# Where weights' forms, probabilities and tokens' forms are made at the change of layer and of batch, in a fused attention and two-layer mixture kernel

## The chip, the cores and the metric

One core of one Trainium2 chip runs the whole kernel in one launch. The metric is device time in microseconds (us). The engines are TensorE (PE; its weight loads are PEld), VectorE (DVE), ScalarE (ACT), GpSimd (POOL) and SyncE (SP), which here issues all DMAs in one queue.

## What is computed

```python
def reference(**kwargs):
    # 2 batches, 8 heads, 768 tokens, 64 per head; local window and global keys
    attn_out = _attn_ref(**attn_kwargs)
    x = attn_out.transpose(0, 2, 1, 3).reshape(B * S, H * D)     # 1536 x 512
    # layer 1: w_gate, w_val 512 x 1536, w_out 1536 x 512
    gate = 1.0 / (1.0 + np.exp(-(x @ w_gate)))
    x = gate * (x @ w_val) @ w_out
    # layer 2: 4 experts, w1 512 x 1024 and w2 1024 x 512 each
    p = domain_probs / (domain_probs.sum(-1, keepdims=True) + 1e-09)
    for e in range(4):
        h = np.maximum(x @ w1[e], 0.0)
        out += p[:, e:e + 1] * (h @ w2[e])
```

## The kernel before

Every float32 product on PE is made of three products of parts: an operand is split into a part rounded to fp32r ("hi", a cast on ACT) and the rest ("lo", a difference on DVE or POOL), and `mm3` (L221) and `mm_on` (L226) multiply hi by hi, hi by lo and lo by hi. Each engine works through its own instructions in the order in which the program issues them; an order is written by hand, in places with generators whose `next` puts one more piece of side work between products.

**Layer 1** (`Experts.run`, L323) has NF // 2 = 6 steps j. In a step, six gates (`gate`, L296: two columns blocks f, three token chunks c of 512) each make 24 products into two banks of PSUM (pg, pv), then a sigmoid on ACT (L309), the gating gf on DVE (L316), its hi on ACT (L319) and lo on POOL (L320). Then twelve second blocks (`second`, L331: three chunks c, four row blocks d) each make six products into a bank po, which DVE adds to `parts` (L345). All of pg, pv and po share the four banks of `ps_mm`. Layer 1's own weights are loaded, decoded and split by `Weights`, a piece at a time ("chores"). In the last step, j = 5, the third chunk (c = 2) is kept for the end: its gates come after the second blocks of the first two chunks, and its four second blocks, a list `last`, are run inside round 0 of layer 2.

**Layer 2** (`Mixed`, L386) works in 32 rounds n: 16 (NG) for each of the two batches, 256 of the experts' columns in each. The product of tokens and w1 is made by a scheme with seven half-size products instead of eight (`PAIRS`, L384: product m takes weight form x and token form y). A round (L529) has seven such products of six matmuls of 384 columns each, on banks a, e and b (b is `o_all`); ACT copies b out twice (s2, L593, and s3, L597) before PE may go on adding into it, and DVE makes c22 (L598) and c12 (L611) from e. Between them stand six token tiles of the round before (`out_tile`, L508: six matmuls of 512 columns, pw, which DVE weighs with the probability and adds up, L524).

- *Weights' forms:* `load` (L406) brings w1's piece ("a") and w2's piece ("b"). `sums` (L414) makes four sums of w1's quarters on DVE (L422), `halves` (L432) splits three pieces into hi (ACT, L435) and lo (POOL or DVE, L436), of 512, 256 and 1024 columns. `outer` (L438) splits w2's piece (ACT, L442; POOL, L443; 1024 columns), which the token tiles of the next round need. In round n >= 1 the forms of round n+1 are made with `ahead`, and `outer(n)` stands near the end.
- *Tokens' forms:* `token_sums` (L449) makes four differences on DVE (L457), `token_form` (L459) splits one form (ACT, L461; DVE or POOL, L462) into a place of `xall`. There are eight places of 768 columns, and seven forms; the places of layer 1's tokens are used again. The forms of batch 0 are made by `begin` (L464) in the last step of layer 1, those of batch 1 inside round 15, each into its old place once the last product of batch 0 that reads it has run.
- *Probabilities:* `token_weights` (L127) loads `pr` (L128) and divides by its sum with four small operations on DVE (L129 to L132).

Before, all of this stood close to the change: at the second-last gate of j = 5 the program issues `load(0)`, `load(1, "a")` and `token_weights`; `begin` puts `sums(0)` behind the first second block of j = 5, then the three pieces, then the token forms; round 0 makes the sums and pieces for round 1 with DVE.

```python
L361  if (f, c) == (NF - 1, 1):
L364      mixed.load(0)
L365      mixed.load(1, "a")
L366      token_weights()
```

Of the kernel before, what the change touches and what calls it, by code (L numbers as in the profile page):

```python
# [18 lines left out]
P = 128  # L19
# [34 lines left out]
def tile_attention_moe(ctx, tc, q, k, v, n_global, n_local, w_gate, w_val, w_out, probs, w1, w2, out):  # L54
# [229 lines left out]
    class Experts:  # L284
# [38 lines left out]
        def run(self):  # L323
# [54 lines left out]
            last = [lambda d=d: (second(NF // 2 - 1, b, NCH - 1, d), next(forms, None)) for d in range(KD)]  # L378
            mixed.run([lambda i=i: [f() for f in last[i:i + 2]] for i in (0, 2)], forms, self.rest)
# [3 lines left out]
    ORDER = (0, 1, 3, 4, 5, 6, 2)  # L383
    PAIRS = {1: (0, 0), 2: (1, 1), 3: (6, 2), 4: (2, 6), 5: (3, 3), 6: (4, 4), 7: (5, 5)}  # L384

    class Mixed:  # L386

# [9 lines left out]

        def more_pools(self):  # L400
# [5 lines left out]
        def load(self, n, which="ab"):  # L406
            e, f0 = divmod(n % NG * 256, F2)
            for x in which:
                src = w1[e, :, f0:f0 + 256] if x == "a" else w2[e, f0:f0 + 256, :]
                t = (wr if n % 2 == 0 else self.rx if x == "a" else self.ry).tile([P, BW], F32, tag="raw", name=f"raw{x}")  # L410
# [3 lines left out]
        def sums(self, n):  # L414
# [8 lines left out]
            pool = self.wf[n % 2]  # L423
            self.forms[n] = [pool.tile([P, 7, KH, P], F32R, tag=x, name=f"w{x}") for x in ("hi", "lo")]
            flat = "p q k f -> p (q k) f"
            self.pieces = [
# [3 lines left out]
            ]  # L430

        def halves(self, i, eng=nc.gpsimd):  # L432

            src, hi, lo = self.pieces[i]
# [24 lines left out]
        def token_form(self, i, eng):  # L459
            hi, lo = (form_slot(i)[:, x] for x in range(2))  # L460
            nc.scalar.copy(hi, self.tsrc[i])  # L461
            eng.tensor_tensor(out=lo, in0=self.tsrc[i], in1=hi.bitcast(F32), op=ALU.subtract)  # L462

        def begin(self, pool):  # L464
# [10 lines left out]
            yield  # L475
            yield
            next(sums)
            self.token_form(3, nc.vector)
            yield
            next(sums)  # L480
            yield
            self.token_form(4, nc.vector)
            yield
            next(sums)
            self.token_form(2, nc.gpsimd)
            yield
            next(sums, None)

            for _ in range(2):
                yield  # L490
            for i in (5, 6):
                yield
                self.token_form(i, nc.vector)

        def product(self, ps, n, m, first):
            x, y = PAIRS[m]
            hi, lo = self.forms[n]
            t = form_slot(y)
# [30 lines left out]
        def round(self, n, fill):  # L529

            b, (s2, s3), (c22, c12) = self.b, *((x[:, :TH] for x in y) for y in (sgs, gfs))
            more = n + 1 < B * NG
            renew = iter(((0, nc.vector), (1, nc.gpsimd), (3, nc.vector), (4, nc.gpsimd), (5, nc.vector), (6, nc.gpsimd), (2, nc.gpsimd))
                         if n % NG == NG - 1 and more else ())
            fill = iter(fill)

            def fills():
                next(fill, lambda: None)()

            def ahead(i, eng=nc.gpsimd):  # L540

                if more and i == 0:
                    self.sums(n + 1)
                if more:
                    self.halves(i, eng)

            def renewed():
                for i, eng in renew:
                    self.token_form(i, eng)
                    break  # L550

            for f in range(2):
# [466 lines left out]
```

## Time and profile before

| what | value |
|---|---|
| median of 3 runs | 925.94 us (925.74 to 927.41) |
| profiled execution, its own time | 925.25 us |
| span, first to last instruction | 923.4 us |
| instructions | 12563 |
| PE busy | 896.4 us, 97% |
| DVE busy | 578.4 us, 63% |
| ACT busy | 393.5 us, 43% |
| POOL busy | 389.5 us, 42% |
| mean granted TensorE clock | 0.990 of full speed |

Busy time counts an instruction from its start to its end, and matmuls overlap one another, so a busy PE is not PE at its peak. A wait is idle time of an engine that ended with an event of another; where several were awaited it is put down to the last. Times in the timeline are counted from the start of the span. Attention and the start of layer 1 take the first 130 us, layer 1 lasts to about 413, with the first products of layer 2 from 402.6, and the change of batch, round 15 to 16, is near 656.

### The profile page before, as it was taken

How to read it: one execution, taken by the hardware profiler on the slowest of the kernel's cores; microseconds unless marked ns; L12 is line 12 of the kernel's file. 1: busy time of each engine (PE TensorE's matmuls, PEld its weight loads, DVE VectorE, ACT ScalarE, POOL GpSimd, SP SyncE). 2: the span in 40 equal slices, each digit the busy share in tenths (PEclk: the TensorE clock that was granted, in tenths of full speed). 3: DMA queues.
4: the chain of work that ended last, by engine and by line, in shares of the span. 5: the costliest groups of instructions: out<-in, count | busy, mean ns of one | idle time of the engine just before them, and what ended most of it. 6: DMA issues, size and time to landing. Idle time of an engine off the chain costs nothing.

```text
span 923.4 us, 12563 instructions
## 1 busy us (share of the span) xinstructions
PE 896.4 (97%) x4736; PEld 771.4 (84%) x4736; DVE 578.4 (63%) x1053; ACT 393.5 (43%) x778; POOL 389.5 (42%) x301
## 2 busy tenths in 40 slices
PE   7989999999999999899999999999899999999997
PEld 5777688888888888688989898989789898989896
DVE  6988653473746465667666666687866666666554
ACT  6989835323232221234343444434443434444331
POOL 2766443333333333333444444445744454444431
PEclk8999999999999999999999999999999999999999
DMA  9633312121121210102212131313132121312102
GB/s 194 155 86 73 109 50 91 46 92 46 65 73 46 92 46 24 46 18 95 72 52 86 46 91 46 92 46 92 57 117 78 47 90 46 92 47 92 46 23 72
DMA packets 83301, 66.46 MB, mean 72 GB/s; under 512 B 43168, under 2 KB 72096, under 8 KB 83232
## 3 DMA queue, kind: packets, MB, share of 16 engines
q1 hardware_dynamic: 83232, 65.57, 24.4%
q8 instruction: 39, 0.64, 0.3%
q14 instruction: 30, 0.25, 0.1%
HBM read 62.42 MB, written 3.15 MB: 71 GB/s over the span
## 4 chain that ended last, share of the span: by engine, by line
PE 87%; DVE 4%; ACT 3%; POOL 2%; issue 2%; DMA 1%; SPq 0%; DVEq 0%; POOLq 0%; ACTq 0%
PE pw L223 9%; PE pw L224 9%; PE pw L222 9%; PE o_all L228 4%; PE o_all L229 3%; PE o_all L230 3%; PE pg L222 3%; PE po L222 3%; PE po L223 3%; PE pv L222 3%; PE po L224 3%; PE pv L224 3%; PE pg L224 3%; PE pv L223 3%; PE pg L223 3%; PE pe L228 2%
## 5 line engine op out<-in xcount | busy, mean ns | idle before, releaser
L524 DVE SCALAR_TENSOR_TENSOR parts<-pw,pr,parts 128x512 f32<-128x512 f32 (+1 forms) x181 | 135.3, 748 | 123.5 <-PE pw L224 123.4
L223 PE MATMUL pw<-olo,h 128*128 128x512 f32 (+1 forms) x386 | 151.5, 393 | 1.4 <-POOL olo L443 1.4
L224 PE MATMUL pw<-ohi,h 128*128 128x512 f32 (+1 forms) x386 | 151.7, 393 | 0.0
L222 PE MATMUL pw<-ohi,h 128*128 128x512 f32 (+1 forms) x386 | 150.5, 390 | 0.0
L443 POOL TENSOR_TENSOR olo<-rawb,ohi 128x1024 fp32r<-128x1024 f32 x32 | 77.2, 2413 | 152.1 <-ACT ohi L442 152.1
L320 POOL TENSOR_TENSOR g<-gf,g 128x512 fp32r<-128x512 f32 x36 | 56.2, 1561 | 135.9 <-ACT g L319 130.7
L436 POOL TENSOR_TENSOR wlo<-sums,whi 128x1024 fp32r<-128x1024 f32 x31 | 74.5, 2402 | 64.6 <-ACT whi L435 64.6
L436 POOL TENSOR_TENSOR wlo<-rawa,whi 128x512 fp32r<-128x512 f32 (+1 forms) x62 | 67.9, 1117 | 64.6 <-ACT whi L435 64.6
L224 PEld LDWEIGHTS pw<-ohi,h 128*128 128x128 f32 x386 | 72.4, 188 | 15.7
L223 PEld LDWEIGHTS pw<-olo,h 128*128 128x128 f32 x386 | 72.6, 188 | 10.8 <-POOL olo L443 2.2
L222 PEld LDWEIGHTS pw<-ohi,h 128*128 128x128 f32 x386 | 72.5, 188 | 8.8
L228 PE MATMUL o_all<-x,whi 128*128 128x384 f32 x194 | 66.3, 342 | 2.7 <-ACT sg L593 2.1
L316 DVE TENSOR_TENSOR gf<-pv,sg 128x512 f32<-128x512 f32 x36 | 24.9, 691 | 66.1 <-PE pv L224 66.1
L229 PE MATMUL o_all<-x,whi 128*128 128x384 f32 x194 | 65.5, 338 | 0.0
L230 PE MATMUL o_all<-x,wlo 128*128 128x384 f32 x194 | 65.4, 337 | 0.0
L505 ACT ACTIVATE h<-gf 128x384 fp32r<-128x384 f32 x64 | 33.7, 527 | 73.3 <-DVE gf L611 52.2
L319 ACT CAST g<-gf 128x512 fp32r<-128x512 f32 x36 | 22.5, 624 | 96.5 <-DVE gf L316 96.5
L806 POOL TENSOR_SCALAR st<-st,rs 128x256 f32<-128x256 f32 (+1 forms) x96 | 48.6, 522 | 34.8 <-DVE rs L799 18.6
L222 PE MATMUL po<-g,whio 128*128 128x512 f32 x144 | 56.9, 395 | 3.4 <-DVE parts L345 2.2
L222 PE MATMUL pg<-x,whig 128*128 128x512 f32 x144 | 57.5, 399 | 0.0
L223 PE MATMUL po<-g,whio 128*128 128x512 f32 x144 | 56.9, 395 | 0.0
L222 PE MATMUL pv<-x,whig 128*128 128x512 f32 x144 | 56.8, 394 | 0.0
(145 smaller groups left out, 2130.9 us busy)
## 6 DMA issues: line engine op xcount, KB each, us to landing
rawa<-in_moe_w_dram SPq DMA_DIRECT2D x32, 512.0 KB, 5.0
rawb<-in_moe_w_dram SPq DMA_DIRECT2D x32, 512.0 KB, 4.0
bitsg<-in_moe_w_gate_dram SPq DMA_DIRECT2D x12, 512.0 KB, 3.7
bitsg<-in_moe_w_val_dram SPq DMA_DIRECT2D x12, 512.0 KB, 4.7
bitso<-in_moe_w_out_dram SPq DMA_DIRECT2D x6, 1024.0 KB, 4.9
v<-in_v_dram SPq DMA_DIRECT2D x12, 256.0 KB, 4.0
out_dram<-parts SPq DMA_DIRECT2D x11, 256.0 KB, 3.0
kn<-in_k_dram SPq DMA_DIRECT2D x10, 256.0 KB, 3.2
```

What stands on the lines that cost most here:

```text
L222: nc.tensor.matmul(ps, ah, bh, start=first, stop=False)
L223: nc.tensor.matmul(ps, ah, bl, start=False, stop=False)
L224: nc.tensor.matmul(ps, al, bh, start=False, stop=last)
L228: nc.tensor.matmul(ps, ah, bh, start=first, stop=False, skip_group_check=True)
L229: nc.tensor.matmul(ps, ah, bl, start=False, stop=False, skip_group_check=True)
L230: nc.tensor.matmul(ps, al, bh, start=False, stop=last, skip_group_check=True)
L320: nc.gpsimd.tensor_tensor(out=g[:, 1], in0=gf, in1=g[:, 0].bitcast(F32), op=ALU.subtract)
L436: eng.tensor_tensor(out=lo, in0=src, in1=hi.bitcast(F32), op=ALU.subtract)
L443: nc.gpsimd.tensor_tensor(out=lo, in0=raw, in1=hi.bitcast(F32), op=ALU.subtract)
L505: nc.scalar.activation(out=hi, in_=of, func=AF.Relu)
L524: nc.vector.scalar_tensor_tensor(out=at, in0=pw, scalar=p_e, in1=at, op0=ALU.mult, op1=ALU.add)
L806: nc.gpsimd.tensor_scalar(out=st, in0=st, scalar1=me["rs"][:, 2 * p + j:2 * p + j + 1], scalar2=1.0, op0=ALU.mult, op1=ALU.mult)
```

## The change

- The DMA of `pr` is issued at the start of `Experts.run`; the four operations on it stand at the start of step j = 1, with the load of the first w1 piece.
- `sums(0)` and the three pieces of round 0 are made in step j = 4, one after each of its first four gates (`begin_weights`). `sums` and `halves` are separated from the allocation of the forms' tiles.
- `begin` then makes only token forms, in another order (0, 1, 4, 3, 2, 5, 6) and a little later, and ends with `sums(1)`.
- The last four second blocks are no longer inside round 0: the two products 1 of round 0 come first (`first_products`), then the second blocks, then `first_round` with an order of products of its own (6, 2, 7, 5, 4, 3), in which the pieces of round 1 are split on ACT and POOL, `outer(0)` stands after the first of them, and the second half of `load(2)` at the end.
- The buffers of w1's and w2's pieces are exchanged: `wr` now holds w2 of even rounds and w1 of odd ones.
- Batch 1's token forms get places shifted by one (`slots`): form 0 goes into the spare eighth place, form 1 into form 0's, and so on along `ORDER`. Their sums are made in rounds 9 to 12 (before: 12 to 15), form 0 in round 13, forms 1, 3, 4 and 5 in round 15 with DVE and 6 and 2 with POOL (before: 0, 3 and 5 with DVE; 1, 4, 6 and 2 with POOL).
- In round 15 `outer` stands right after the first product, not near the end.

```diff
     def token_weights():
-        nc.sync.dma_start(out=pr, in_=probs.rearrange("(t p) e -> p t e", p=P))
         nc.vector.tensor_reduce(prs, pr, AX.X, ALU.add)
...
+            nc.sync.dma_start(out=pr, in_=probs.rearrange("(t p) e -> p t e", p=P))
             for j in range(NF // 2):
                 final = j == NF // 2 - 1
+                if j == 1:
+                    token_weights()
+                    mixed.load(0, "a")
+                early = mixed.begin_weights() if j == NF // 2 - 2 else iter(())
                 for f in fs:
                     for c in range(NCH - final):
                         if (f, c) == (NF - 1, 1):
...
-                            mixed.load(0)
+                            mixed.load(0, "b")
                             mixed.load(1, "a")
-                            token_weights()
                         gates(f, c, self.weights.chore)
+                        next(early, None)
...
-            last = [lambda d=d: (second(NF // 2 - 1, b, NCH - 1, d), next(forms, None)) for d in range(KD)]
-            mixed.run([lambda i=i: [f() for f in last[i:i + 2]] for i in (0, 2)], forms, self.rest)
+            mixed.first_products()
+            for d in range(KD):
+                second(NF // 2 - 1, b, NCH - 1, d)
+                next(forms, None)
+            for _ in forms:
+                pass
+            self.rest.close()
+            mixed.run()
...
+            order = (7,) + self.ORDER
+            self.slots = [{i: i for i in self.ORDER}, {i: order[k] for k, i in enumerate(self.ORDER)}]
...
-                t = (wr if n % 2 == 0 else self.rx if x == "a" else self.ry).tile(...)
+                t = (wr if (n % 2 == 0) == (x == "b") else self.rx if x == "a" else self.ry).tile(...)
...
+        def begin_weights(self):
+            self.sums(0)
+            for i in range(3):
+                yield
+                self.halves(0, i)

         def begin(self, pool):
             sums = self.token_sums(0, pool, "bits")
             next(sums)
-            self.sums(0)
+            for _ in range(3):
+                yield
+            self.token_form(0, 0, nc.vector)
             yield
-            for i in range(3):
-                self.halves(i)
+            self.token_form(0, 1, nc.vector)
+            for _ in range(3):
                 yield
-            self.token_form(0, nc.vector)
-            self.token_form(1, nc.vector)
...
+            for i in (None, 4, 3, None, 2):
+                if i is None or i == 4:
+                    next(sums, None)
+                if i is not None:
+                    self.token_form(0, i, nc.gpsimd if i == 2 else nc.vector)
+                yield
...
+            self.sums(1)
...
+        def first_round(self):
+            a, e = self.first
+            self.more_pools()
+            self.load(1, "b")
+            self.load(2, "a")
+            self.halves(1, 0)
+            self.outer(0)
+            self.product(b, 0, 6, False)
+            nc.scalar.copy(s2, b)
+            self.product(a, 0, 2, False)
+            self.gated(0, 0, 0, a, nc.vector)
+            self.halves(1, 2)
+            self.product(b, 0, 7, False)
+            nc.scalar.copy(s3, b)
+            self.product(e, 0, 5, True)
+            nc.vector.tensor_tensor(out=c22, in0=e, in1=s3, op=ALU.add)
+            self.product(b, 0, 4, False)
+            self.gated(0, 1, 0, b, nc.vector)
+            self.halves(1, 1)
+            self.product(e, 0, 3, False)
...
+            self.load(2, "b")
...
         def round(self, n):
-            renew = iter(((0, nc.vector), (1, nc.gpsimd), (3, nc.vector), (4, nc.gpsimd), (5, nc.vector), (6, nc.gpsimd), (2, nc.gpsimd))
-                         if n % NG == NG - 1 and more else ())
+            renew = iter(zip(self.ORDER[1:], (nc.vector,) * 4 + (nc.gpsimd,) * 2) if n == NG - 1 else ())
...
             self.product(a, n, 1, True)
+            nc.scalar.copy(b, a)
+            if n == NG - 1:
+                self.outer(n)
             renewed()
             fills()
...
-            if n == NG - 4:
+            if n == NG - 7:
                 self.sums_ahead = self.token_sums(1, self.ts, "ts")
                 next(self.sums_ahead)
-            if NG - 4 <= n < NG:
+            if NG - 7 <= n < NG - 3:
                 next(self.sums_ahead, None)
+            if n == NG - 3:
+                self.token_form(1, 0, nc.vector)
...
-            if n:
+            if n != NG - 1:
                 self.outer(n)
```

## Rows read from the trace of the kernel before

**Rows 1.** The page, part 1: busy time, share of the span, instructions.

```profile
PE 896.4 (97%) x4736; PEld 771.4 (84%) x4736; DVE 578.4 (63%) x1053; ACT 393.5 (43%) x778; POOL 389.5 (42%) x301
```

**Rows 2.** PE's waits, whole span: releaser: us in total, times, longest.

```profile
PE po L222 <- DVE parts L345: 2.2, 1, 2.2
PE o_all L228 <- ACT sg L593: 2.1, 2, 1.1
...
PE pw L223 <- POOL olo L443: 1.4, 1, 1.4
...
PE po L222 <- DVE gf L316: 1.2, 1, 1.2
...
PE o_all L228 <- ACT sg L597: 0.6, 1, 0.6
PE pe L228 <- DVE gf L598: 0.4, 1, 0.4
```

**Rows 3.** Windows: stretch, its length, busy (x instructions) by engine, granted clock, DMA share, GB/s.

```profile
150.00:200.00 50.00, 50.00 (x222) 41.42 (x221) 22.99 (x29) 17.29 (x28) 16.83 (x9) 1.00 0.20 64
304.51:326.28 21.77, 21.77 (x98) 18.03 (x97) 9.28 (x10) 6.26 (x9) 7.21 (x4) 1.00 0.16 50
375.23:391.71 16.48, 13.08 (x49) 9.99 (x48) 12.52 (x21) 4.08 (x6) 6.46 (x5) 0.90 0.20 55
385.00:390.00 5.00, 4.11 (x11) 3.23 (x12) 5.00 (x8) 2.62 (x3) 2.39 (x1) 0.68 0.00 0
391.71:402.60 10.89, 10.89 (x50) 9.01 (x49) 7.79 (x10) 4.13 (x6) 4.23 (x2) 1.00 0.01 2
402.60:404.72 2.12, 2.12 (x13) 2.12 (x12) 0.69 (x1) 1.10 (x2) 0.40 (x1) 1.00 0.00 0
412.52:419.56 7.04, 5.03 (x25) 4.07 (x24) 6.80 (x10) 4.66 (x8) 2.37 (x1) 1.00 0.74 227
623.83:641.96 18.13, 18.13 (x92) 16.34 (x90) 13.64 (x19) 7.49 (x14) 7.27 (x5) 1.00 0.25 67
639.52:660.73 21.21, 18.71 (x91) 16.22 (x90) 19.08 (x22) 12.44 (x21) 15.51 (x9) 1.00 0.17 52
```

**Rows 4.** Timeline of SP's DMA queue, 372 to 380: start, us, engine, line.

```profile
373.98 0.51 SPq L128 DMA_DIRECT2D pr<-in_moe_domain_probs_dram  x1
```

**Rows 5.** Timeline of DVE, 372 to 388; in brackets idle time before, and releaser.

```profile
379.05 0.20 DVE L129 TENSOR_REDUCE prs<-pr 128x12 f32<-128x48 f32 x1 [5.43 <-DMA pr<-in_moe_domain_probs_dram]
...
379.89 0.69 DVE L316 TENSOR_TENSOR gf<-pv,sg 128x512 f32<-128x512 f32 x1
...
381.08 0.42 DVE L422 TENSOR_TENSOR sums<-rawa 128x256 f32<-128x256 f32 x1
...
385.15 2.54 DVE L345 TENSOR_TENSOR parts<-po,parts 128x512 f32<-128x512 f32 x5
```

**Rows 6.** Timeline of POOL, 636 to 655.

```profile
637.40 2.41 POOL L443 TENSOR_TENSOR olo<-rawb,ohi 128x1024 fp32r<-128x1024 f32 x1 [4.53 <-ACT ohi L442]
...
648.78 2.44 POOL L436 TENSOR_TENSOR wlo<-sums,whi 128x1024 fp32r<-128x1024 f32 x1 [1.77 <-ACT whi L435]
651.18 2.57 POOL L462 TENSOR_TENSOR x<-tsum,x 128x768 fp32r<-128x768 f32 x1
```

**Rows 7.** Timeline of DVE, 640 to 653.

```profile
642.01 0.96 DVE L462 TENSOR_TENSOR x<-parts,x 128x768 fp32r<-128x768 f32 x1 [1.07 <-ACT x L461]
...
647.22 0.41 DVE L422 TENSOR_TENSOR sums<-rawa,sums 128x256 f32<-128x256 f32 x1
...
649.54 2.49 DVE L457 TENSOR_TENSOR tsum<-parts,tsum 128x768 f32<-128x768 f32 x1
```

**Rows 8.** Timeline of ACT in round 0.

```profile
412.49 1.05 ACT L442 CAST ohi<-rawb 128x1024 fp32r<-128x1024 f32 x1 [3.10 <-PE po L223]
```

**Rows 9.** Timeline of ACT in round 15.

```profile
641.14 0.84 ACT L461 CAST x<-parts 128x768 fp32r<-128x768 f32 x1
```

**Rows 10.** The page, part 5: line, engine, operation, busy and mean ns, idle before.

```profile
L524 DVE SCALAR_TENSOR_TENSOR parts<-pw,pr,parts 128x512 f32<-128x512 f32 (+1 forms) x181 | 135.3, 748 | 123.5 <-PE pw L224 123.4
```

More of the change, by code (lines that the diff above doesn't have):

```diff
@@ L527, in out_tile, with ahead @@
                     nc.sync.dma_start(out=out[row:row + P, ds], in_=at)
-        def round(self, n, fill):
-            b, (s2, s3), (c22, c12) = self.b, *((x[:, :TH] for x in y) for y in (sgs, gfs))
-            more = n + 1 < B * NG
-            renew = iter(((0, nc.vector), (1, nc.gpsimd), (3, nc.vector), (4, nc.gpsimd), (5, nc.vector), (6, nc.gpsimd), (2, nc.gpsimd))
-                         if n % NG == NG - 1 and more else ())
-            fill = iter(fill)
-            def fills():
[L538 to L545, printed above, removed]
+        def ahead(self, n, i, eng=nc.gpsimd):
+            if n < B * NG:
+                if i == 0:
+                    self.sums(n)
+                self.halves(n, i, eng)
@@ new lines, in banks, with first_products @@
+        def banks(self, n):
+            for f in range(2):
+                self.h[n, f] = self.hp[n % 2].tile([P, 2, TB], F32R, tag="h", name="h")
+            return [ps_t.tile([P, C], F32, tag="t", name=x)[:, :TH] for x in ("pa", "pe")]
+        def first_products(self):
+            self.first = self.banks(0)
+            self.product(self.first[0], 0, 1, True)
+            self.product(self.b, 0, 1, True)
+        def first_round(self):
+            b, (s2, s3), (c22, c12) = self.b, *((x[:, :TH] for x in y) for y in (sgs, gfs))
+            a, e = self.first
[17 more added lines that the diff above has]
+            self.product(e, 0, 3, False)
+            nc.vector.tensor_tensor(out=c12, in0=e, in1=s2, op=ALU.add)
+            self.gated(0, 0, 1, c12, nc.vector)
+            self.gated(0, 1, 1, c22, nc.vector)
+            self.load(2, "b")
@@ L547, in renewed, with round @@
+        def round(self, n):
+            b, (s2, s3), (c22, c12) = self.b, *((x[:, :TH] for x in y) for y in (sgs, gfs))
+            renew = iter(zip(self.ORDER[1:], (nc.vector,) * 4 + (nc.gpsimd,) * 2) if n == NG - 1 else ())
+            fill = iter(range(TT))
+            def fills():
+                self.out_tile(n - 1, next(fill))
             def renewed():
                 for i, eng in renew:
-                    self.token_form(i, eng)
+                    self.token_form(1, i, eng)
@@ L550, in renewed @@
                     break
-            for f in range(2):
-                self.h[n, f] = self.hp[n % 2].tile([P, 2, TB], F32R, tag="h", name="h")
-            a = ps_t.tile([P, C], F32, tag="t", name="pa")[:, :TH]
-            e = ps_t.tile([P, C], F32, tag="t", name="pe")[:, :TH]
+            a, e = self.banks(n)
             self.product(a, n, 1, True)
-            if n == 0:
-                self.product(b, n, 1, True)
-            else:
-                nc.scalar.copy(b, a)
+            nc.scalar.copy(b, a)
@@ L573, in round @@
             renewed()
[L574 to L575 removed]
+            self.ahead(n + 1, 2)
             fills()
[L577 to L587 removed]
+            if n == NG - 7:
                 self.sums_ahead = self.token_sums(1, self.ts, "ts")
                 next(self.sums_ahead)
[L590 removed]
+            if NG - 7 <= n < NG - 3:
                 next(self.sums_ahead, None)
+            if n == NG - 3:
+                self.token_form(1, 0, nc.vector)
             self.product(b, n, 6, False)
@@ L614, in round, with run @@
             self.gated(n, 0, 1, c12, nc.vector)
-        def run(self, fill, forms, rest):
-            self.rest, self.first = rest, forms
-            for n in range(B * NG):
-                self.round(n, fill)
-                fill = [lambda n=n, t=t: self.out_tile(n, t) for t in range(TT)]
-            for tile_out in fill:
-                tile_out()
+        def run(self):
+            self.first_round()
+            for n in range(1, B * NG):
+                self.round(n)
+            for t in range(TT):
+                self.out_tile(B * NG - 1, t)
     def head_rows(src, b, s0, n):
```

64 lines of the change are left out of this document (19 added, 45 removed).

## The prediction, made before the change was timed

> **What bounds the kernel now.** I read the shares of busy time first: PE is busy for 97% of the span [rows 1], so only time in which PE stands still, or runs slowly, can be won. The list of PE's waits says where it stands [rows 2]: leaving the attention aside, its entries name one of two places, the change of layer (releasers L345, L316, L593, L597, L598) and the change of batch (L593 once more, L443). Then I cut the span into stretches whose work can be compared [rows 3]. From 375.23 to 391.71 PE issues the 48 products of eight second blocks; from 391.71 to 402.60 it issues 48 products of the same size without a gap, in 10.89 us. The first stretch took 16.48, so 5.59 us are lost in it: 1.2 and 2.2 of waiting [rows 2], and 2.2 mostly in products at a lowered clock, since after the two gaps the granted clock shows 0.68 of full speed between 385 and 390, a mix of the levels 1.2 and 2.4 GHz [rows 3]. In round 0, the 24 products from 412.52 to 419.56 took 7.04; 12 of that size took 2.12 at 402.60, so 24 need 4.24 and 2.80 are lost. At the change of batch I compare 639.52 to 660.73, which is round 15 with the first product and token tile of round 16, with 623.83 to 641.96, the same work one round earlier: 21.21 against 18.13, so 3.08 are lost [rows 3]. Together 11.5 us can be won at these two places, and no more.
>
> **Change of layer, the probabilities.** The DMA of pr is issued at 373.98 [rows 4]; DVE, which has the reduction of pr next in its order, stands idle for 5.43 until it has landed at 379.05 [rows 5]. Behind it stands gf L316, whose bank of PSUM PE wants: the wait of 1.2. The change issues this DMA ahead of layer 1, on SP with nothing there to wait for, and the four small operations at the start of its second step (j = 1). They take 0.84, from 379.05 to the next operation at 379.89 [rows 5], and in 150 to 200, which holds the start of j = 1, DVE is busy 22.99 of 50 while PE never stands [rows 3]: I cost them at nothing. Without that cover they would cost at most their 0.84.
>
> **Change of layer, the weights' sums and forms.** Four sums run on DVE from 381.08 to 385.15, and the additions L345 that free PE's banks stand behind them [rows 5]: the wait of 2.2. They move, with three casts on ACT and three differences on POOL, behind the first four gates of j = 4. Those gates, 304.51 to 326.28, leave DVE busy 9.28 and POOL 7.21 of 21.77 [rows 3], so the sums' 4.07 and about 4.3 on POOL (an estimate by columns, 1792 against 1024 in the 2.44 of [rows 6]) find room. What queues behind them are weights of the second blocks, which begin two gates after this stretch, at 337. I cost the move at nothing; without cover, 4.07. What is late next in 375 to 391? DVE has eight additions left and three passes over 768 columns, which stand singly between additions; PE has four banks, so a delay of 0.96 [rows 7] reaches no product. Both gaps go, and with them the low clock: 5.59. Bounds 3.4, if the clock falls for other reasons, and 5.6.
>
> **Change of layer, round 0.** The new order makes two first products, four second blocks, then the other products, with the weight pieces of round 1 made on POOL instead of DVE and their sums made before. PE's first wait in the old round was for the copy s2 L593, behind the casts L442 and L435 on ACT; L442 itself had waited 3.10 for PE's last second block, whose memory it takes over [rows 8]. It still does. But s2 now stands behind that one cast of 1.05 [rows 8], and PE has two products (b6 and a2, 2.12) before b7 needs the copy. So about 0.2 remains of the 2.80; bounds 0 and 0.6 (the cast of a piece, if it waits for the same memory). Saved: 2.6. The layer change gives 5.6 + 2.6 = 8.2, bounds 5.6 and 8.4.
>
> **Change of batch, what goes.** The token sums move from rounds 12 to 15 to rounds 9 to 12, and form 0 to round 13, into the spare place. Round 14 carried such a pass with PE busy 18.13 of 18.13 [rows 3]: nothing. The shifted places let each form be made one product earlier; no row shows PE waiting for a form: nothing. Outer(15) moves to the head of round 15, so olo is ready when round 16 asks for it: the wait of 1.4 [rows 2] goes.
>
> **Change of batch, what comes.** The outer's cast now stands on ACT ahead of the cast of form 1, and its difference on POOL ahead of everything. Before, the first form's cast began at 641.14 and its difference ran on DVE from 642.01 to 642.97 [rows 7, 9]. Now the outer's cast (1.05) begins there, form 1's cast ends at about 642.9, and POOL has begun the outer's difference, 2.41 long [rows 6], at 642.25. What DVE does meanwhile is seen at 649.54: a subtraction of two SBUF operands, of the size that takes 0.96, took 2.49 and ended at 652.03, 0.81 after POOL's operation of 648.78 had ended at 651.22 [rows 6, 7]. So form 1's difference ends at 644.66 + 0.81 = 645.5, 2.5 later than its counterpart. A token tile (0.75 [rows 10]) and the sums for round 16 follow. Before, the sums ended at 647.63 [rows 7], with a form on POOL among them that is gone now; I take about 1.7 back for it and put their end at 648.55, 0.9 later. Their cast and s2 stand behind them on ACT, so PE's wait of 1.1 for s2 [rows 2] grows to about 2.1, and product b7 starts at 650.0.
>
> A second wait comes new. After the sums DVE has a gated difference, forms 3 and 4, a tile, form 5, a tile, then c22, for which product e3 waits. POOL's piece (2.44) and its form 6 (taken as 2.0; 2.57 at 651.18 with a wait in it [rows 6]) fall between these. From 648.55: 0.5 + 0.9, blocked to 652.4, 0.8 + 0.7, blocked to 655.1, then 0.8 + 0.7 + 0.5 gives 657.0 (operations of 384 columns at half of 0.96). PE, from 650.0, has two products of 1.06 and two tiles of 1.36 [rows 3] and wants c22 at 654.9: another 2.1. So round 15 loses about 4.3 against 3.08 before: **+1.2**. Bounds: 1.2 lost in all, if the sums end as before and DVE's forms get ahead of POOL's work, and 4.3: a gain of 1.9 and a loss of 1.2.
>
> The Trainium skill, SBUF — State Buffer, section "SBUF: two separate sides", says that a DVE operation with two SBUF inputs and a GpSimd operation exclude each other for a whole instruction, whichever starts first. The trace agrees, by the 0.81 above. By that rule the earlier outer on POOL speaks against the change, at +1.2; if the two only shared the port, form 1's difference would at most double, end by 644.0, and both waits would stay under 1: the change of batch would gain about 1.
>
> **The sum.** The profiled execution took 925.25 us (span 923.4): 925.25 - 8.2 + 1.2 = 918.25. It lies 0.69 below the median of the runs, 925.94, so I give 918.9.
>
> **The rivals.**
> 1. DVE gets ahead: at POOL's ends its waiting operations run back to back, so c22 is in time and only s2 is late. For it: the subtraction of 649.54 went before POOL's operation of 651.18 [rows 6, 7]. Against: POOL asks before form 4 does. Round 15 then loses 2.2, or 2.1 less than forecast: 916.8.
> 2. The clock falls in round 15. Two waits of over 2 us, five apart, resemble the 1.2 and 2.2 after which it showed 0.68; against: from 412.52 to 419.56 PE was idle for 2.0 of 7.04 and the clock stayed at 1.00 [rows 3]. Price: what the layer change lost beyond its waits, 2.2: 921.1.
> 3. Slower: the same fall, but the clock stays at 1.2 GHz. Each microsecond so spent does half its work, so a low stretch of over 18 us, longer than a round, eats the 7.0 saved and 1.9 more. Two rounds, 31 us of work, would cost 31: 950. Nothing here lasted so: from 391.71 on the clock shows 1.00 again [rows 3].
> 4. The change doesn't do what it says: the early casts wait on ACT for memory still in use, and sigmoids behind them hold PE. Against: additions and sums of these forms ran at 381 [rows 5], with layer 1 still working. Two gaps like the old ones with their clock cost 5.6: 924.5.
>
> **Chances.** Forecast 0.55, rival 1 0.22, rival 2 0.12, rival 4 0.06, rival 3 0.05. A measurement of this kernel can tell about 0.2%, 1.9 us, from no change. Faster takes the first three, 0.89; same is rival 4, 0.06; slower is rival 3, 0.05. The range reaches from the best bounds of both places (8.4 + 1.9 = 10.3 saved: 915.6) to rival 2 with the 1.5 by which the slowest run of before lies above its median: 922.6. It holds the first three cases.
>
> **What would show it.** Right: no PE wait for L316 or L345 at the layer change, the granted clock at 1.00 there, pr's DMA near the end of the attention, the sums of round 0 near 311, the wait for L443 gone; at the change of batch, form 1's difference ending 0.8 after POOL's outer, a PE wait for s2 and one for c22 of about 2 each. Wrong: a PE wait in the steps j = 1 or j = 4, a clock under 1.00 after round 15, or a change of batch that loses nothing.

## The result, and the profile after

The changed kernel takes 917.50 us (median of 4 runs, 917.02 to 919.04) against 925.97 (4 runs, 925.74 to 927.41): a ratio of 0.9908, with a 95% interval of 0.9891 to 0.9925. The forecast was 918.9, in a range of 915.6 to 922.6. The profiled execution took 917.02 us with a span of 915.2, 8.2 us less span than before.

The page of the kernel after, part 1, in the columns of [rows 1]:

```profile
PE 893.9 (98%) x4736; PEld 772.1 (84%) x4736; DVE 580.2 (63%) x1052; ACT 392.4 (43%) x778; POOL 390.4 (43%) x302
```

The work is the same but for one operation, now on POOL and not on DVE; PE's share of the span rose by a point because the span is shorter. PE's waits after, in the columns of [rows 2]:

```profile
PE tq L668 <- DVE pt L860: 6.3, 4, 2.0
PE o_all L227 <- ACT sg L633: 1.9, 1, 1.9
PE tp L853 <- POOL st L843: 1.6, 3, 0.7
PE o_all L101 <- POOL ident masks.py:199: 1.4, 1, 1.4
...
PE s_ps L684 <- DVE mn L816: 1.3, 1, 1.3
```

All lines but the second belong to the attention or the start. Of the entries of [rows 2], 7.9 us in all, one is left in both layers: the wait for s2 (now L633) in round 15, grown from 1.1 to 1.94. In the windows of the kernel after (columns as in [rows 3]) the first is the last step of layer 1, from its first second block to round 1, and the second five microseconds out of it; the third is round 15 up to the second product of round 16, and the fourth five microseconds out of that (its clock, 0.68, is a mix of the levels 1.2 and 2.4 GHz):

```profile
374.01:409.96 35.95, 35.95 (x170) 30.87 (x169) 24.36 (x36) 13.04 (x20) 12.95 (x8) 1.00 0.17 49
385.00:390.00 5.00, 5.00 (x24) 4.14 (x23) 3.65 (x6) 2.05 (x3) 0.00 (x0) 1.00 0.00 0
629.96:652.00 22.04, 20.11 (x92) 17.42 (x91) 18.70 (x22) 11.54 (x20) 11.82 (x8) 0.92 0.15 48
640.00:645.00 5.00, 4.57 (x16) 4.01 (x17) 5.00 (x4) 2.33 (x5) 4.30 (x2) 0.68 0.00 0
```

The first is PE without a gap, at full clock, in 35.95 us. The same window of the kernel before took 44.33, at a mean clock of 0.96:

```profile
375.23:419.56 44.33, 38.92 (x169) 31.75 (x168) 32.63 (x47) 15.48 (x24) 14.36 (x9) 0.96 0.19 57
```

The third holds what is still lost: 22.04 for work that takes 18.13 undisturbed [rows 3], so 3.91, against 3.08 before. I cut both spans at the same products in PE's timeline, to see where each microsecond of the 8.2 came from (lengths in us):

| stretch | before | after | difference |
|---|---|---|---|
| attention: from the start to the first second block of layer 1 | 141.31 | 140.09 | -1.22 |
| to the first second block of step j = 5 | 233.92 | 233.92 | 0.00 |
| **change of layer**: to round 1 | 44.33 | 35.95 | -8.38 |
| to round 15 | 219.96 | 220.00 | +0.04 |
| **change of batch**: to the second product of round 16 | 21.21 | 22.04 | +0.83 |
| to round 31 | 233.26 | 233.25 | -0.01 |
| to the end of PE's last product | 24.38 | 24.33 | -0.05 |
| to the end of the span | 5.08 | 5.65 | +0.57 |

The first and the last row are scatter: over the thirteen profiles of this study the attention took 140.0 to 142.1 us and the tail 5.1 to 5.7, with no relation to what was edited. Between them, stretches of the same code repeat within 0.05 from profile to profile, but for one stretch in one experiment, which is named there. So the table by stretch tells edits apart that the medians of whole runs can't, and every experiment below is read by it. It holds for the one profiled execution of each kernel.

### The profile page after: what moved, and what is told of

It reads as the page before. It is cut to its first block, busy times and chain, and to the rows that moved or that the text cites. A ratio compares the mean times of both kernels' runs of the same rounds, so it can differ in the third digit from the quotient of the medians.

```text
span 915.2 us, 12567 instructions
## 1 busy us (share of the span) xinstructions
PE 893.9 (98%) x4736; PEld 772.1 (84%) x4736; DVE 580.2 (63%) x1052; ACT 392.4 (43%) x778; POOL 390.4 (43%) x302
## 4 chain that ended last, share of the span: by engine, by line
PE 90%; ACT 3%; DVE 3%; issue 2%; POOL 1%; DMA 0%; SPq 0%; DVEq 0%; POOLq 0%; ACTq 0%
PE pw L222 10%; PE pw L223 10%; PE pw L221 10%; PE o_all L227 4%; PE o_all L228 4%; PE o_all L229 4%; PE po L222 4%; PE po L223 4%; PE po L221 4%; PE pg L221 3%; PE pg L223 3%; PE pg L222 3%; PE pv L221 3%; PE pv L223 3%; PE pv L222 3%; PE pe L227 2%
## 5 line engine op out<-in xcount | busy, mean ns | idle before, releaser
L459 POOL TENSOR_TENSOR olo<-rawb,ohi 128x1024 fp32r<-128x1024 f32 x32 | 77.0, 2406 | 149.9 <-ACT ohi L458 149.9
L452 POOL TENSOR_TENSOR wlo<-sums,whi 128x1024 fp32r<-128x1024 f32 x32 | 77.8, 2433 | 64.3 <-ACT whi L451 64.3
L452 POOL TENSOR_TENSOR wlo<-rawa,whi 128x512 fp32r<-128x512 f32 x64 | 71.1, 1131 | 61.4 <-ACT whi L451 58.9
L222 PE MATMUL po<-g,whio 128*128 128x512 f32 x144 | 56.2, 390 | 0.0
L223 PE MATMUL pg<-x,wlog 128*128 128x512 f32 x144 | 56.1, 390 | 0.0
```

The costliest lines, as they stand in the source:

```text
L222: nc.tensor.matmul(ps, ah, bl, start=False, stop=False)
L223: nc.tensor.matmul(ps, al, bh, start=False, stop=last)
L452: eng.tensor_tensor(out=lo, in0=src, in1=hi.bitcast(F32), op=ALU.subtract)
L459: nc.gpsimd.tensor_tensor(out=lo, in0=raw, in1=hi.bitcast(F32), op=ALU.subtract)
```

## The experiments

Each edit is made to the changed kernel; ratios are to the kernel before, run beside it. **Two questions:** which part of the change gives the 8.4 us at the change of layer, and what makes the 3.9 us still lost at the change of batch.

### The layer's part alone, and the batch's part alone

The first undoes the change of batch: the old places, sums in rounds 12 to 15, outer(15) late.

```diff
-            self.slots = [{i: i for i in self.ORDER}, {i: order[k] for k, i in enumerate(self.ORDER)}]
+            self.slots = [{i: i for i in self.ORDER}, {i: i for i in self.ORDER}]
...
-            renew = iter(zip(self.ORDER[1:], (nc.vector,) * 4 + (nc.gpsimd,) * 2) if n == NG - 1 else ())
+            renew = iter(zip(self.ORDER, (nc.vector, nc.gpsimd) * 3 + (nc.gpsimd,)) if n == NG - 1 else ())
...
-            if n == NG - 1:
-                self.outer(n)
...
-            if n == NG - 7:
+            if n == NG - 4:
...
```

> Theory: the layer change alone carries the gain (8.4 us in its stretch) and the batch change costs 0.8. Then round 15 loses 3.1 us again, with waits of about 1.1 for s2 and 1.4 for olo and the clock at 1.00, and the time is about 916.7 us, under that of the whole change. Rival: the batch change holds a part of the gain; then the time is 918 us or more.

Measured: 917.67 us (5 runs, 915.96 to 918.38), ratio 0.9903 (0.9887 to 0.9920). Its windows of the two places:

```profile
375.88:411.79 35.91, 35.91 (x170) 30.86 (x168) 24.32 (x36) 13.04 (x20) 12.91 (x8) 1.00 0.15 48
631.78:652.96 21.18, 18.69 (x92) 16.20 (x90) 19.06 (x22) 12.42 (x21) 15.48 (x9) 1.00 0.11 27
```

The layer's stretch is that of the changed kernel, the batch's that of the kernel before (21.21), with its two waits, 1.1 for s2 and 1.4 for olo (the lo of w2's piece, which `outer` makes). So the new order of round 15 costs 22.04 - 21.18 = 0.86. The medians, 917.67 and 917.50, don't show that: the attention took 141.96 in this profile and 140.09 in the other.

The second undoes the layer's part: pr and its four operations, the sums and pieces of round 0, and round 0's own order go back. The early load of the first w1 piece and the exchanged buffers stay.

```diff
-            nc.sync.dma_start(out=pr, in_=probs.rearrange("(t p) e -> p t e", p=P))
...
-                    token_weights()
                     mixed.load(0, "a")
-                early = mixed.begin_weights() if j == NF // 2 - 2 else iter(())
+                early = iter(())
...
                             mixed.load(1, "a")
+                            nc.sync.dma_start(out=pr, in_=probs.rearrange("(t p) e -> p t e", p=P))
+                            token_weights()
...
             mixed.first_products()
-            for d in range(KD):
...
```

> Theory: the layer change's 8.4 us are lost again, and round 15 loses 3.9 us as in the changed kernel (a wait of 1.9 for s2, granted clock 0.68 after it): about 926.8 us, 0.8 over the kernel before. Rival: the batch change is worth something by itself; then the time is under 925 us.

Measured: 923.82 us (12 runs, 922.28 to 925.30), ratio 0.9976 (0.9965 to 0.9988). It was to be slower than before and is faster. The rival's time came, but not for its reason: the change of batch took 22.07, against 21.21 before, and so earns nothing by itself; the layer's stretch took 41.54 and not 44.33:

```profile
374.46:416.00 41.54, 37.38 (x169) 30.62 (x168) 33.49 (x47) 15.24 (x24) 13.90 (x9) 1.00 0.17 46
385.00:390.00 5.00, 4.84 (x22) 3.74 (x21) 5.00 (x9) 0.44 (x1) 1.34 (x1) 1.00 0.00 0
```

The wait for gf is gone, and so is the low clock of [rows 3]; one wait of 2.0 for L344 (before: L345) is left. Something that I had kept, and not priced, was worth 2.8 us here. The DMA of pr gives the trace of it. Here it landed 3.9 us after its issue and in the kernel before 5.1: its reduction ended DVE's idle time after 3.75 us where [rows 5] has 5.43. What stands in SP's queue ahead of it differs; in the kernel before:

```profile
355.52 0.37 SPq L412 DMA_DIRECT2D rawa<-in_moe_w_dram  x1
373.05 0.37 SPq L412 DMA_DIRECT2D rawb<-in_moe_w_dram  x1
373.46 0.47 SPq L412 DMA_DIRECT2D rawa<-in_moe_w_dram  x1
```

Two loads of w pieces go just ahead of pr; with the exchanged buffers rawb gets a free one at 354.75 and only one load stands there, at 372.28.

### The batch's part alone, with the old loads and buffers

This experiment puts the loads and buffers back as well. To the edit above it adds:

```diff
-                t = (wr if (n % 2 == 0) == (x == "b") else self.rx if x == "a" else self.ry).tile([P, BW], F32, tag="raw", name=f"raw{x}")
+                t = (wr if n % 2 == 0 else self.rx if x == "a" else self.ry).tile([P, BW], F32, tag="raw", name=f"raw{x}")
...
-                    mixed.load(0, "a")
+                    pass
...
-                            mixed.load(0, "b")
+                            mixed.load(0)
```

> As the batch change alone, but with the loads and buffers of the kernel before, so that pr follows two loads of 512 KB and not one in SP's queue. Theory: pr lands about 1.2 us later (5.1 against 3.9 after its issue), the wait for gf of 1.2 returns, with it the low clock, and the last step to round 1 takes 44.3 as in the kernel before, against 41.5. Rival: the order of the token forms is what made the difference; then it stays at 41.5.

Measured: 925.75 us in one run, with the kernel before at 923.68 beside it (one run; over seventeen other runs it took 923.65 to 927.84). The layer's stretch is back at 44.28, and with it the two waits and the clock. Its windows, and the entries of its waits that belong there:

```profile
374.31:418.59 44.28, 38.95 (x170) 31.77 (x168) 33.39 (x47) 15.35 (x24) 13.95 (x9) 0.96 0.19 56
385.00:390.00 5.00, 5.00 (x15) 3.96 (x16) 4.95 (x6) 1.92 (x3) 2.40 (x1) 0.66 0.00 0
```

```profile
PE po L221 <- DVE parts L344: 2.2, 1, 2.2
...
PE po L221 <- DVE gf L315: 1.1, 1, 1.1
PE o_all L227 <- ACT sg L582: 1.0, 1, 1.0
PE o_all L227 <- ACT sg L584: 0.6, 1, 0.6
PE pe L227 <- DVE gf L585: 0.4, 1, 0.4
```

pr was issued 0.5 later in the stretch, behind the second load, took 5.0 us to land, and DVE idled 5.40 for it. So, with pr loaded late, the exchange of buffers with the loads in two places is worth 44.28 - 41.54 = 2.74: 1.1 of waiting for gf, and nearly all the rest the products at a lowered clock (PE is busy 38.95 instead of 37.38).

### One layer edit undone at a time

First pr late, with its four operations behind `load(1, "a")`; then the sums and pieces of round 0 late, in `begin`:

```diff
-                early = mixed.begin_weights() if j == NF // 2 - 2 else iter(())
+                early = iter(())
...
             next(sums)
-            for _ in range(3):
+            self.sums(0)
+            for i in range(3):
                 yield
+                self.halves(0, i)
             self.token_form(0, 0, nc.vector)
```

> Theory of the prediction: with the load of the probabilities and its four operations back at the second-last gate, DVE idles over 5 us for it and PE waits 1.2 for gf; the last step to round 1 takes 37.1 or more. Rival, from the batch change alone: with one load ahead of it in SP's queue and not two, pr lands about 1.2 us sooner and the wait all but vanishes: under 36.3.

> Theory: with the sums and pieces of round 0 back between the second blocks, the four sums hold up DVE's additions and PE waits 2.0 to 2.3 us once. Whether the low clock (2.2 more) comes with one such wait decides between 38.2 (no) and 40.4 (yes) for the last step to round 1; the batch change alone showed a wait of 2.0 without it, so 38.2 is likelier.

Measured (one run each): 917.89 and 918.20 us. The layer's stretch took 35.92 with pr late, as the rival had it, so that edit alone is worth nothing. It took 36.34 with the weights late, worth 0.4: both times that I had named, 38.2 and 40.4, were wrong, and PE has no wait for L344 at all. With pr late DVE does stand idle for it (timeline of DVE; in brackets idle time before):

```profile
376.91 0.20 DVE L128 TENSOR_REDUCE prs<-pr 128x12 f32<-128x48 f32 x1 [3.71 <-DMA pr<-in_moe_domain_probs_dram]
...
377.74 0.69 DVE L315 TENSOR_TENSOR gf<-pv,sg 128x512 f32<-128x512 f32 x1
378.34 1.88 DVE L344 TENSOR_TENSOR parts<-po,parts 128x512 f32<-128x512 f32 x3
```

gf comes late and the additions run back to back, three in 1.88, but PE never waits: its banks take up the lateness. Then both late together, and then round 0 alone in its old order (second blocks inside it, DVE making the pieces of round 1):

```diff
             mixed.first_products()
-            for d in range(KD):
-                second(NF // 2 - 1, b, NCH - 1, d)
-                next(forms, None)
...
-            mixed.run()
+            mixed.run([lambda d=d: (second(NF // 2 - 1, b, NCH - 1, d), next(forms, None)) for d in range(KD)], forms, self.rest)
...
+            self.sums(1)
+            self.halves(1, 0, nc.vector)
+            self.halves(1, 1, nc.vector)
             self.product(b, 0, 6, False)
...
```

> Theory, formed after the two edits alone cost 0.0 and 0.4: DVE's lateness is the sum of the wait for pr and of the weights' sums, and PE waits only for what exceeds its four banks. With both back and the loads in the changed order, the last step to round 1 takes 38.5 to 39.0 (2.8 over the 35.9 of the changed kernel), most of it one wait for L344. Rival: the two are independent; then it takes 36.4.

> Theory: the old order of round 0 alone, with sums and pieces of round 1 on DVE inside it, brings back the waits for the two copies and c22 (1.0, 0.6, 0.4) and costs 2.6 to 2.8: the last step to round 1 takes 38.6. Rival: round 0 is also coupled to what stands before it; then it takes under 37.5.

Measured (one run each): 921.32 and 919.80 us. The layer's stretch of the two, the first from the kernel with both late, the second from that with the old round 0:

```profile
375.97:414.63 38.66, 36.62 (x169) 30.73 (x168) 30.26 (x44) 14.70 (x23) 17.62 (x11) 1.00 0.17 47
```

```profile
373.93:412.65 38.72, 36.74 (x169) 30.79 (x168) 27.55 (x39) 13.57 (x21) 9.19 (x6) 1.00 0.14 48
```

Both late cost 38.66 - 35.93 = 2.73 (35.93 is the stretch in the changed kernel's second profile, from 374.06 to 409.99), nearly seven times what the two cost alone, 0.0 and 0.4: a wait of 1.9 for L344, as DVE is late by pr and then holds the additions behind the sums, more than PE's banks take up. The old round 0 costs 2.79, with the three waits of before, 1.0, 0.6 and 0.4. The waits of the two kernels, both late first:

```profile
PE po L221 <- DVE parts L344: 1.9, 1, 1.9
```

```profile
PE pe L227 <- DVE gf L638: 1.4, 1, 1.4
...
PE o_all L227 <- ACT sg L580: 1.0, 1, 1.0
PE o_all L227 <- ACT sg L582: 0.6, 1, 0.6
PE pe L227 <- DVE gf L583: 0.4, 1, 0.4
```

(L638 is c22 of round 15, of which more below.) Now the 8.4 us is accounted for: 2.74 (buffers and loads) + 2.73 (pr and weights) + 2.79 (round 0) = 8.26 of 8.38. Put in one after another, from the old loads on, the stretch goes 44.28, 41.54 (buffers and loads), 38.66 (round 0), 35.93 (pr and weights), which is 8.35. The shares hold for this order of edits: the 2.74 was measured with pr late, and no run puts the old buffers beside an early pr.

### The change of batch: the outer late, the cast behind the copy

Two edits, each against one suspect of the wait for s2. In the first outer(15) goes back to its late place; in the second it stays, and ACT casts the sums of the weights behind the copy s2 instead of ahead of it.

```diff
             nc.scalar.copy(b, a)
-            if n == NG - 1:
-                self.outer(n)
...
-            if n != NG - 1:
-                self.outer(n)
+            self.outer(n)
```

```diff
-            self.ahead(n + 1, 2)
+            if n != NG - 1:
+                self.ahead(n + 1, 2)
...
             nc.scalar.copy(s2, b)
+            if n == NG - 1:
+                self.ahead(n + 1, 2)
```

> Theory: the early outer in round 15 holds the port for 2.4 us and so delays form 1 on DVE, the sums, their cast and s2. With outer back at its place late in the round, form 1's difference ends about 2.4 us earlier against the start of the round, the wait for s2 falls from 1.9 to under 1 and the clock stays at 1.00; a wait for olo of 1 to 2 us comes back, behind forms 6 and 2 on POOL. Round 15 loses about 2 us in place of 3.9: about 915.6 us. Rival: the number of forms on DVE is the cause, not the place of outer; then the wait for s2 stays at 1.9 or more and the time is 917.5 us or more.

> Theory: the last link of the chain is ACT's order, in which the cast of the sums stands before the copy s2. With that cast behind s2 in round 15 alone, the wait for s2 goes, the clock stays at 1.00 and the wait for c22 that the low clock had hidden appears, up to 2.2 us. Round 15 loses about 2.2 us: about 915.8 us. Rival: the clock falls in round 15 whatever PE waits for; then it still shows about 0.68 there and the round loses 3.5 us or more.

Measured: 920.24 us (4 runs, 919.14 to 920.47), ratio 0.9932 (0.9914 to 0.9950), and 919.92 (4 runs, 918.93 to 920.75), ratio 0.9935 (0.9917 to 0.9954). Neither gained what I expected; both medians lie above that of the changed kernel. PE's waits in these stretches, with the outer late and then with the cast behind:

```profile
PE pw L222 <- POOL olo L459: 2.2, 1, 2.2
...
PE pe L227 <- DVE gf L636: 1.4, 1, 1.4
```

```profile
PE pe L227 <- DVE gf L641: 3.1, 1, 3.1
...
PE o_all L227 <- ACT sg L640: 0.2, 1, 0.2
```

With the cast behind, the wait for s2 fell to 0.2, and the one for c22 (L641) grew to 3.1: the stretch took 22.03, as in the changed kernel (22.04), with the clock at 1.00. That is the loss of the rival, without its fall of the clock. c22 begins 648.28 - 631.82 = 16.46 us after the stretch's start; in the changed kernel 16.45. So DVE's order of work up to c22 sets the end, and the wait for s2 lies inside it. The timeline of DVE, with the outer late and then with the cast behind:

```profile
645.68 0.54 DVE L636 TENSOR_TENSOR gf<-pe,sg 128x384 f32<-128x384 f32 x1
```

```profile
648.28 0.54 DVE L641 TENSOR_TENSOR gf<-pe,sg 128x384 f32<-128x384 f32 x1
```

This profile of the cast behind is of its fastest run, 918.93. The other three took 919.26 to 920.75, more than any of the changed kernel's nine runs (917.02 to 919.18), at a mean clock of 0.987 to 0.991 against 0.993 in the profiled one; where they lost the time, no profile shows.

With the outer late, c22 begins 645.68 - 631.45 = 14.23 after the start, 2.2 earlier, so the early outer on POOL holds DVE by that much; but POOL then reaches the outer behind form 6, and PE waits 2.2 for olo. The timeline of POOL in that kernel:

```profile
647.96 1.86 POOL L478 TENSOR_TENSOR x<-parts,x 128x768 fp32r<-128x768 f32 x1 [3.68 <-ACT x L477]
649.78 2.66 POOL L459 TENSOR_TENSOR olo<-rawb,ohi 128x1024 fp32r<-128x1024 f32 x1
```

PE comes to c22 earlier as well and still waits 1.4 for it. The stretch took 22.65, and the one behind it, to round 31, 1.2 more than the 233.25 of the others, with a granted clock of 0.82 from 655 to 660. Given the new shares of DVE and POOL in the forms, the early outer therefore earns 22.65 + 1.2 - 22.04 = 1.8; it only doesn't pay for the shares.

### The forms spread out

If DVE's work ahead of c22 is the limit, forms have to leave that stretch, and POOL's have to lie where DVE has no two-operand work from SBUF. Form 1 stays on DVE at the head of round 15; then come form 4 on POOL, form 3 on DVE in an extra place ahead of product b7, and form 5 on POOL; forms 6 (DVE) and 2 (POOL) go into round 16, whose last products are the first to read them. The outer is late.

```diff
-            renew = iter(zip(self.ORDER[1:], (nc.vector,) * 4 + (nc.gpsimd,) * 2) if n == NG - 1 else ())
+            at = {(NG - 1, 0): (1, nc.vector), (NG - 1, 3): (4, nc.gpsimd), (NG - 1, 4): (3, nc.vector), (NG - 1, 5): (5, nc.gpsimd),
+                  (NG, 0): (6, nc.vector), (NG, 5): (2, nc.gpsimd)}
+            places = iter(range(8))
...
-                for i, eng in renew:
+                i, eng = at.get((n, next(places)), (None, None))
+                if eng is not None:
                     self.token_form(1, i, eng)
-                    break
...
-            if n == NG - 1:
-                self.outer(n)
...
             fills()
+            renewed()
             self.product(b, n, 7, False)
...
-            if n != NG - 1:
-                self.outer(n)
+            self.outer(n)
```

> Theory, as the runs so far leave it: what ends round 15 late is the order of DVE, which reaches c22 16.5 us after the round's start, both in the changed kernel and with the cast behind s2; the wait for s2 and the low clock lie inside that. Here the shifted places are used to spread the forms: in round 15 form 1 on DVE at the start, 3 on DVE before product b7, 4 and 5 on POOL; in round 16 form 6 on DVE at the start and 2 on POOL; outer at its usual place. Then c22 comes about 13 us after the start, no wait of PE over 0.5 us is left at the change of batch, the stretch that took 22.0 takes 18.2 to 18.8, and the time is 913.5 to 914.3 us. Rival: the places bring nothing, since the same operations collide with POOL wherever they stand; then the waits move into round 16 and the stretch with round 16 loses 2 us or more.

> The changed kernel once more beside the one with the forms spread, on the same chip: every theory expects 917.5 us, within 1.2, with 35.9 us from the first second block of the last step to round 1 and 22.0 from round 15 to the second product of round 16. If the layer change is worth 8.4 and the batch change costs 0.8, the mean of all its runs lies 0.8 above that of the layer change alone, which the scatter of the attention (about 1 us) may hide.

Measured: 913.62 us (4 runs, 913.33 to 915.23), ratio 0.9872 (0.9857 to 0.9887). The changed kernel itself, run again beside it: 918.03 (5 runs, 917.17 to 919.18), ratio 0.9924 (0.9910 to 0.9937). The windows of the kernel with spread forms:

```profile
375.85:411.77 35.92, 35.92 (x170) 30.87 (x168) 24.34 (x36) 13.04 (x20) 12.92 (x8) 1.00 0.15 47
631.77:650.14 18.37, 18.37 (x92) 16.29 (x91) 13.99 (x21) 10.50 (x18) 12.16 (x7) 1.00 0.11 31
```

In the timeline of DVE, c22:

```profile
642.52 0.54 DVE L639 TENSOR_TENSOR gf<-pe,sg 128x384 f32<-128x384 f32 x1
```

PE has no wait left at the change of batch. c22 begins 642.52 - 631.77 = 10.75 after the start, 5.7 earlier than in the changed kernel and earlier than the 13 that I had expected, DVE is busy 13.99 instead of 18.70, and the stretch is within 0.24 of the undisturbed 18.13. This version beats both kernels.

## Why the prediction was right, and where it was not

**The whole.** The sum gave 918.25 for the profiled execution, which took 917.02. Of the 1.23 between, 0.18 is the change of layer (-8.38 for -8.2), 0.37 the change of batch (+0.83 for +1.2), and the rest, 0.68, nearly all the scatter of attention and tail in the table, on which the forecast had no hold.

**Change of layer: the total held, its shares did not.** I gave 1.2 to pr, 2.2 to the sums and 2.2 to the clock, one price per edit, from the waits of [rows 2]. Undone alone in the changed kernel, pr costs 0.0 and the weights 0.4; together 2.7. The exchange of buffers with the split load, listed as part of the change and not costed by me, is worth 2.7 while pr is late: it makes pr land sooner, and so takes the wait that I had put to pr's move. The edits overlap, and none has one price; what the buffers are worth once pr is early, and what the move of pr alone gives with the old buffers, was not run. The step that failed is taking the releaser of a wait for an edit's price: DVE's lateness adds up over pr's landing, four operations and four sums, and PE's four banks take up part of it once, whoever caused it. The sum held because the losses of a stretch, 5.59 read from its own length, don't depend on how they are shared out, and the change happened to undo every cause at once, the one that I had not seen included. To that extent it was luck.

**The cover I named.** pr's DMA is issued at 119.66, its four operations, the first of step j = 1 in DVE's order, run from 149.9, while PE still has second blocks of j = 0, and the sums for round 0 in step j = 4:

```profile
309.61 0.42 DVE L437 TENSOR_TENSOR sums<-rawa 128x256 f32<-128x256 f32 x1
310.06 0.42 DVE L437 TENSOR_TENSOR sums<-sums,rawa 128x256 f32<-128x256 f32 x1
310.41 0.42 DVE L437 TENSOR_TENSOR sums<-rawa 128x256 f32<-128x256 f32 x1
310.74 1.52 DVE L437 TENSOR_TENSOR sums<-rawa,sums 128x256 f32<-128x256 f32 x1
```

They end at 312.3, and PE waits in neither step: the stretch from the first second block to step j = 5 took 233.92 before and after. "Near 311" was right. The four operations on pr took some 2.7 us there, since the last of them ran 2.03, and not the 0.84 of [rows 5]; PE didn't wait for them.

**Round 0.** Priced at 2.6 of the 2.80, measured at 2.79 by putting the old order back. The 0.2 that I let remain didn't come: PE doesn't wait for s2 in round 0.

**Change of batch: the first wait.** The chain through the outer, form 1, the sums and their cast came as written. The timeline of DVE in the changed kernel:

```profile
633.40 2.54 DVE L478 TENSOR_TENSOR x<-parts,x 128x768 fp32r<-128x768 f32 x1 [2.02 <-ACT x L477]
...
638.51 0.41 DVE L437 TENSOR_TENSOR sums<-rawa,sums 128x256 f32<-128x256 f32 x1
...
639.32 4.00 DVE L478 TENSOR_TENSOR x<-tsum,x 128x768 fp32r<-128x768 f32 x2
...
643.90 1.92 DVE L478 TENSOR_TENSOR x<-tsum,x 128x768 fp32r<-128x768 f32 x1
...
646.41 0.54 DVE L638 TENSOR_TENSOR gf<-pe,sg 128x384 f32<-128x384 f32 x1
```

and of POOL beside it:

```profile
632.71 2.41 POOL L459 TENSOR_TENSOR olo<-rawb,ohi 128x1024 fp32r<-128x1024 f32 x1 [2.46 <-ACT ohi L458]
...
640.08 2.42 POOL L452 TENSOR_TENSOR wlo<-sums,whi 128x1024 fp32r<-128x1024 f32 x1 [2.11 <-ACT whi L451]
643.13 1.88 POOL L478 TENSOR_TENSOR x<-tsum,x 128x768 fp32r<-128x768 f32 x1 [0.62 <-ACT x L477]
```

and the first matmul of product b7 on PE, with its wait for s2:

```profile
640.43 0.44 PE L227 MATMUL o_all<-x,whi 128*128 128x384 f32 x1 [1.94 <-ACT sg L633]
```

Counted from the start of round 15 (639.52 before, 629.96 after), form 1's difference was to end at 5.98 and ended at 5.98; the sums at 9.03, and they ended at 8.96; b7 was to start at 10.48 and started at 10.47. Three times a difference on DVE ends 0.81 to 0.82 after POOL's operation beside it: 635.94 after 635.12, 643.32 after 642.50, 645.82 after 645.01. The Trainium skill, SBUF — State Buffer, section "SBUF: two separate sides", has a DVE operation with two SBUF inputs and a GpSimd operation exclude each other for a whole instruction. By that rule I had put the change of batch at +1.2, and by sharing at a gain of about 1. The trace agrees with the rule, by these three ends and at +0.83, and the experiment with the outer late, in which c22 comes 2.2 earlier, agrees too.

**The second wait, mis-sized.** I had c22 done at 17.5 and PE there at 15.4, a wait of 2.1. It was done at 16.99, as POOL's piece and form ended 0.5 earlier in all than I had them. In the profile shown first there is no such wait, but the clock showed 0.68 from 640 to 645, and PE came to c22 as it was done. In the profile with round 0's old order, whose round 15 is the same code, the clock stayed at 1.00, and PE waited 1.44. Both stretches took the same, 22.04 and 22.05. The loss is set by c22, and shows as a low clock or as a wait. The wait's size was wrong, 1.44 for 2.1, and so was the total: 3.91 lost for 4.3.

**The rivals.** The first, DVE ahead of POOL's work, is out: DVE was held each time. The second, a fall of the clock in round 15, happened and cost nothing, since its price lay inside the wait for c22; my 2.2 was taken from the change of layer, where no later wait took it up. The third and the fourth did not come: from 650 on the clock shows 1.00 again in the changed kernel, and no cast held PE in j = 4.

## What to carry to other kernels

Price a stretch by its own length against undisturbed work, and only then share the loss out; undoing one edit at a time can understate each, where buffers take up the first lateness for free, so undo pairs too. Before buying off a wait, look what is late next on the same engine: moving the cast away took 1.7 off the wait for s2 and put 1.7 on the wait for c22 (3.1 for the 1.4 of the profiles whose clock stayed at 1.00), and only taking work off DVE ahead of c22 shortened the round. And where a buffer is exchanged, follow the DMA queue: a load that no longer waits for its buffer changes what a small transfer behind it has to wait for.

## What the runs showed of the hardware that I had not expected

- **The granted clock doesn't follow the waits alone.** After the same wait of 1.9 for s2, in the same code of round 15, it showed 0.66 to 0.70 over the next five microseconds in four profiles (the changed kernel, the same again, pr late, both late) and 1.00 in four others (both with the batch's part alone, weights late, the old round 0); after a wait of 3.1 (cast behind) it stayed at 1.00, and after 1.4 and 2.2 (the outer late) it showed 0.82 from 655 to 660. What decides it, no run here tells. In none of the eight did the stretch differ: 22.02 to 22.07.
- **A small DMA can take over a microsecond longer behind two loads than behind one.** pr, 24 KB, landed 5.0 to 5.1 us after its issue behind two loads of w pieces of 512 KB (two profiles), and 3.8 to 3.9 behind one (three). It isn't the only cause: issued early, behind loads of layer 1's weights, it took 4.3 to 5.8 in eight profiles with the same order of loads.
- **The attention's length scatters by 2 us** from one profile to another (140.0 to 142.1), and so does one and the same kernel's whole time (917.02 to 919.18), which is why differences under 1 us are read here from stretches and not from medians. It doesn't explain all scatter: seventeen runs of the kernel before spread over 4.2 us (923.65 to 927.84), and where the rest of that lies no profile shows.
